# Retention and gated MLP on one core: mask and query scale built on the chip, two groups' totals interleaved with the next scores, one written order for all engines

## The chip, the cores and the metric

One core of one Trainium2 chip. The metric is the device time of one execution in microseconds (us); lower is better. TensorE (PE in the rows, its weight loads PEld) multiplies matrices, VectorE (DVE), ScalarE (ACT) and GpSimd (POOL) work on elements, SyncE (SP) issues the loads.

## The reference

For 4 batches, 8 heads, 768 positions and head size 64, a retention layer, then a gated MLP:

```python
for t in range(S):
    state = gamma * state + k[t] (outer) v[t]
    y[t] = (1 / sqrt(D)) * q[t] @ state
x = heads of y side by side                      # [4, 768, 512]
h = relu(x @ w_in); u, v = h[:512], h[512:]
v_n = (v - mean(v)) / sqrt(var(v) + 1e-6)
v_s = w_spatial @ v_n + b_spatial                # over positions
out = (u * v_s) @ w_out
```

All of it is wanted in float32 precision; the kernel gets it from pairs of float32r numbers (a high part and a residue), three products for one.

## The kernel before, in words

**Retention.** The 768 positions of a batch are 6 groups of 128; 4 batches give groups 0 to 23. A group has two halves i of 64 positions, and its 8 heads lie as 4 pairs, the two heads of a pair on partitions 0 to 63 and 64 to 127. `load_group` (L261) loads keys and queries (tile `qk`, 3 buffers), `load_values` (L273) values and natural keys (`vk`, 2 buffers; for groups 2, 5 and 8 `third`). `scale_values` (L289) multiplies the values by a decay from `vd_t`, in one POOL instruction or in 8 of ACT. `ret_scores` (L330) makes scores s = k'q in 16 products of 64x64, each two matmul records; `ret_mask` (L337, DVE) applies the causal mask `mask_t`. `total_sum` (L303) adds k'v of a half to a running total in PSUM (tile `total`, 8 products, 16 records), and `total_copy` (L318, ACT) copies the total to `states`. `out_products` (L381) makes x from scores and state (64 records for a group), `out_evict` (L408, DVE) takes it from PSUM in 4 instructions with the query scale `qg_t`, `qd_t`; `out_half` makes the high part `xh` (ACT) and the residue `xl` (POOL or DVE). x of groups 0 to 5 is written to the pool `ps_o`, whose three banks also hold the total. After group 5, `ret_set` (L342) alternates the scores of the next group with the update of the state, without a running total.

**MLP.** `v_products` (L456) makes v for one group and one quarter of the weights (3 matmuls of 512 columns), then `v_relu`, `v_stats`, `v_power`, `v_bias`, `mlp_norm` give the normalised `vn` (ACT, DVE, POOL). `mlp_u` (L579) makes u (12 matmuls), `spatial_products` (L598) multiplies vn by w_spatial (tile `sp`), `mlp_out` (L641) makes the output. Batch 0 multiplies in plain or split form, batches 1 to 3 by seven products (`product`, L540).

**Weights.** Twelve blocks of float64 words (L0 to L3 for v, L4 to L7 for u, L8 to L11 for the output) are loaded by `load_double` (L146) and taken apart: `split_top` on ACT, five DVE instructions (L181 to L204), `split_high` on ACT, `split_residue` (two instructions, POOL or DVE). Blocks 3 to 11 are staged in rooms that they share: L9 takes the room of L4.

**Order.** `START` (L24) is a string of words; while it is emitted, every instruction of every engine keeps this order. A word is a step and a number: q scores, j mask, p scale, t total, k copy, y output products, E eviction, h and l the halves of x, V products for v, r s w n N the norm, u, P spatial, G, L, K loads, a c H R the taking apart of a weight block. p23 scales group 3 on ACT, p1 group 1 on POOL. `FIRST`, `REST` and `LAST` (L37 to L57) give the order of batches 0 to 3; there only PE, the loads and the weight splits keep it, and a planner orders the rest. Before `START` ten matmuls on zeros run (`WARM_UP`, L738).

Of the kernel before, what the change touches and what calls it, by code (L numbers as in the profile page):

```python
# [9 lines left out]
F32 = mybir.dt.float32  # L10
# [13 lines left out]
START = (  # L24
# [10 lines left out]
)  # L35
FIRST = (
    "S6 W0 I4 W1 D1 X6 J9 S7 G9 D2 I5 X7 J10 G10 D3 W2 S8 W3 I6 X8 S9 V0 G11 W4 I7 X9 J11 S10 "  # L37
    "G12 O7 N0 X10 W5 V1 V2 V3 N1 N2 J12 G13 S11 X11 J13 G14 V4 N3 S12 N4 V5 W6 N5"
)
REST = (  # L40
# [4 lines left out]
)  # L45
LAST = (
    "U0 U2 C01 U4 C05 U6 C06 U1 U3 C03 M01 C07 M05 C02 M06 C04 M03 M07 M02 C11 M04 C15 F0 F2 O0 "
    "C16 O2 U5 U7 C13 M11 C17 M15 C12 M16 C14 M13 M17 M12 M14 F1 F3 O1 F4 O3 F6 O4 F5 O6 F7 O5 "
    "O7"
)  # L50


STAGED = {3: 0, 4: 1, 5: 2, 6: 3, 7: 4, 8: 0, 9: 1, 10: 2, 11: 3}
ROOMS = (12, 13)
# [769 lines left out]
```

## Time and profile before

| | us |
|---|---|
| median of 3 runs (lowest, highest) | 375.12 (374.98, 376.07) |
| span of the profiled execution, first to last instruction | 372.8 |
| PE busy in the span | 362.0 |
| DVE / ACT / POOL busy | 236.4 / 154.5 / 134.4 |

The profile gives one execution by its span; what lies around the span is known only as the difference of 2.3 us to the median. PE is the busiest engine by far, so the time is PE's work plus the time in which PE waits or runs at a lower clock. The chain that ended last, the windows (busy time of each engine in a stretch, with the granted clock) and the waits show where those are.

### The profile page before, as it was taken

How to read it: one execution, taken by the hardware profiler on the slowest of the kernel's cores; microseconds unless marked ns; L12 is line 12 of the kernel's file. 1: busy time of each engine (PE TensorE's matmuls, PEld its weight loads, DVE VectorE, ACT ScalarE, POOL GpSimd, SP SyncE). 2: the span in 40 equal slices, each digit the busy share in tenths (PEclk: the TensorE clock that was granted, in tenths of full speed). 3: DMA queues.
4: the chain of work that ended last, by engine and by line, in shares of the span. 5: the costliest groups of instructions: out<-in, count | busy, mean ns of one | idle time of the engine just before them, and what ended most of it. 6: DMA issues, size and time to landing. Idle time of an engine off the chain costs nothing.

```text
span 372.8 us, 10291 instructions
## 1 busy us (share of the span) xinstructions
PE 362.0 (97%) x4418; PEld 317.3 (85%) x4418; DVE 236.4 (63%) x513; ACT 154.5 (41%) x308; POOL 134.4 (36%) x131
## 2 busy tenths in 40 slices
PE   6899999999999999999999999999999999999996
PEld 2778785787998878999998888999997888999985
DVE  3989989995887876677674543367674433165530
ACT  2486682264433535533124444432323445432232
POOL 1354650001343523526424451327424341325042
PEclk9899999999999999999999999999999999999999
DMA  7997783001431721113305332021504002000022
GB/s 265 411 371 278 243 310 156 0 2 54 147 114 58 273 89 69 54 61 109 122 2 199 114 114 86 8 106 47 185 0 143 2 2 86 0 0 2 0 86 85
DMA packets 13581, 41.49 MB, mean 111 GB/s; under 512 B 1888, under 2 KB 2144, under 8 KB 13536
## 3 DMA queue, kind: packets, MB, share of 16 engines
q1 hardware_dynamic: 13392, 40.71, 30.0%
q8 instruction: 35, 0.57, 0.6%
q10 hardware_dynamic: 144, 0.13, 0.1%
q14 instruction: 10, 0.08, 0.1%
HBM read 34.54 MB, written 6.29 MB: 110 GB/s over the span
## 4 chain that ended last, share of the span: by engine, by line
PE 94%; DMA 3%; issue 1%; DVE 1%; POOL 0%; SPq 0%; ACT 0%; POOLq 0%
PE u L126 18%; PE v L126 18%; PE o L126 18%; PE y L126 10%; PE sp L126 8%; PE x L126 7%; PE z L126 5%; PE s L126 3%; PE d L126 3%; PE w L126 3%; DMA qk<-in_groups_dram 2%; DMA vd_t<-in_vdecay_dram 2%; PE total L126 1%; PE o_last L126 0%; POOL vk L298 0%
## 5 line engine op out<-in xcount | busy, mean ns | idle before, releaser
L126 PE MATMUL u<-xh,winu_w 128*128 128x384 f32 x256 | 68.1, 338 | 0.0
L126 PE MATMUL v<-winv_w,xh 128*128 128x512 f32 x192 | 60.6, 397 | 0.2 <-issue 0.2
L126 PE MATMUL o<-wout_w,gh 128*128 128x512 f32 (+1 forms) x192 | 60.5, 396 | 0.0
L126 PEld LDWEIGHTS u<-xh,winu_w 128*128 128x128 f32 x256 | 46.5, 188 | 0.8
L126 PE MATMUL u<-xl,winu_w 128*128 128x384 f32 x128 | 42.9, 335 | 0.0
L134 POOL TENSOR_TENSOR xl<-xf,xh 128x512 fp32r<-128x512 f32 x21 | 29.0, 1380 | 37.6 <-ACT xh L436 37.6
L126 PEld LDWEIGHTS v<-winv_w,xh 128*128 128x128 f32 x192 | 35.2, 188 | 8.1 <-issue 0.4
L126 PE MATMUL y<-sp,a 128*128 128x384 f32 x216 | 41.6, 336 | 0.0
L126 PEld LDWEIGHTS o<-wout_w,gh 128*128 128x128 f32 x192 | 35.2, 188 | 7.3
L534 ACT CAST a<-vn 128x384 fp32r<-128x384 f32 x42 | 21.6, 513 | 46.0 <-PE y L126 16.9
L134 POOL TENSOR_TENSOR gl<-ur,gh 128x384 fp32r<-128x384 f32 x24 | 26.8, 1116 | 37.7 <-ACT gh L630 37.2
L134 DVE TENSOR_TENSOR a<-vn,a 128x384 fp32r<-128x384 f32 x42 | 24.4, 580 | 24.6 <-ACT a L534 24.2
L126 PEld LDWEIGHTS y<-sp,a 128*128 128x128 f32 x216 | 38.1, 188 | 0.2
L126 PE MATMUL v<-winv_w,xl 128*128 128x512 f32 x96 | 37.5, 390 | 0.0
L126 PE MATMUL o<-wout_w,gl 128*128 128x512 f32 (+1 forms) x96 | 37.3, 389 | 0.0
L477 DVE BATCH_NORM_STATS2 bst<-vr 128x6 f32<-128x512 f32 x24 | 16.6, 691 | 29.3 <-ACT vr L470 29.1
L419 DVE SCALAR_TENSOR_TENSOR xf<-x,qg_t,qd_t 128x128 f32<-128x128 f32 x96 | 27.1, 343 | 10.3 <-PE x L126 10.3
L484 POOL TENSOR_TENSOR rs<-rs,mhalf 128x1 f32<-128x1 f32 x24 | 13.7, 573 | 44.0 <-DVE rs L479 41.8
L126 PE MATMUL s<-qk 64*64 64x64 f32 x768 | 27.4, 221 | 0.7 <-DMA qk<-in_groups_dram 0.7
L126 PEld LDWEIGHTS s<-qk 64*64 64x64 f32 x768 | 25.1, 137 | 2.9 <-DMA qk<-in_groups_dram 1.4
L500 ACT ACTIVATE vn<-vr,nb,rs 128x512 f32<-128x512 f32 x24 | 19.4, 814 | 17.4 <-DVE nb L489 16.4
L595 ACT ACTIVATE ur<-u 128x384 f32<-128x384 f32 x32 | 15.7, 490 | 25.9 <-PE u L126 25.7
(103 smaller groups left out, 669.8 us busy)
## 6 DMA issues: line engine op xcount, KB each, us to landing
qk<-in_groups_dram SPq DMA_DIRECT2D x24, 512.0 KB, 5.3
vk<-in_groups_dram SPq DMA_DIRECT2D x21, 512.0 KB, 4.4
out_dram<-ot SPq DMA_DIRECT2D x23, 256.0 KB, 2.1
wst<-in_w_sp_dram SPq DMA_DIRECT2D x4, 576.0 KB, 8.1
raw<-in_w_inv_dram SPq DMA_DIRECT2D x4, 512.0 KB, 6.5
raw<-in_w_inu_dram SPq DMA_DIRECT2D x4, 512.0 KB, 7.5
raw<-in_w_out_dram SPq DMA_DIRECT2D x4, 512.0 KB, 5.1
third<-in_groups_dram SPq DMA_DIRECT2D x3, 512.0 KB, 6.0
```

The lines of the kernel that those rows point to most:

```text
L126: ins = nc.tensor.matmul(out, lhs, rhs, start=start, stop=stop, skip_group_check=shared)
L134: return eng.tensor_tensor(out, whole, high.bitcast(F32), ALU.subtract)
L419: nc.vector.scalar_tensor_tensor(xf[:, hp], t[hp % 2][:, hp // 2].rearrange("p i c -> p (i c)"), qg_t[:, c, hp : hp + 1], qd_t[:, hp], ALU ...
L477: keep(nc.vector.bn_stats(st, norm[b, c][0]))
L484: keep(nc.gpsimd.tensor_tensor(rs, rs, mhalf, ALU.pow))
L500: keep(nc.scalar.activation(vn[b][:, c], v, AF.Identity, bias=nb, scale=rs))
L534: nc.scalar.copy(t[:, 0], whole)
L595: keep(nc.scalar.activation(u, pu[:, :HALF], AF.Relu))
```

## The change

Mask: built by POOL (memset and two affine selects) instead of loaded. Query scale: two rows are loaded, spread over 128 partitions by one float32 matmul with a 0/1 matrix, and copied by ACT (m2, m0, m1) instead of loaded whole (256 KB). `vd_t` and `qg_t` come in one load. Totals of groups 3 and 4 alternate with the scores of groups 4 and 5 (t130, t131, t140, t141). The total is written on the other half of the partitions and copied by two instructions of 64 partitions (k000, k001, ...). Filler matmuls on zeros: 11 at the start and eight more between steps (words U). Functions of several instructions are cut into steps of one engine each, and one string, `STEPS`, orders every instruction of the whole kernel; no planner is left. Numbers of the words change (p202: group 2 on ACT; R100: first residue instruction of block 0 on DVE; Q0: its second on POOL; E00: first eviction of group 0; x600: one addition to the state). From the v products of group 12 on, PE's order is that of before; ahead of it, in batch 0, it is changed.

```diff
-    "L0 G0 a0 c00 c01 H0 v c02 m q0 L2 j0 p0 t00 k00 y00 y01 t01 R20 G1 L1 p1 a2 G2 c20 E0 q1 "
-    "h0 k01 c21 j1 t10 y10 a1 H2 k10 G3 c10 y11 p22 t11 c22 q2 c11 k11 c12 L3 l0 H1 q3 t20 k20 "
-    "E1 G4 R1 V00 j2 h1 t21 l11 p23 k21 y20 y21 L5 R2 j3 q4 t30 E2 a3 h2 j4 c30 V10 p24 V01 V11 "
-    "V02 L4 l12 c31 V20 a5 k30 y30 c32 t31 H3 k31 c50 G5 y31 q5 E3 t40 a4 j5 R3 V21 V12 k40 c40 "
...
+    "U10 U301 G0 v q0 U201 j0 m2 m0 L0 a0 c00 c01 c02 p0 t00 m1 k000 k001 y00 U101 G1 p1 q1 "
+    "j1 H0 c03 R100 t01 y01 U501 E00 E02 c04 E01 Q0 E03 k010 k011 t10 k100 k101 t11 U401 U701 "
+    "U601 L1 a1 c10 L2 y10 G2 k110 k111 a2 y11 c11 c20 c21 E10 c22 q2 j2 c12 E12 E11 E13 p202 "
+    "t20 U801 k201 k200 c13 c14 h0 l0 G3 t21 H2 k210 k211 G4 h1 l101 H1 R101 p203 y20 y21 E20 "
+    "E21 Q1 q3 j3 c23 t130 k301 V00 V10 V11 k300 t131 E23 E22 p204 k310 k311 j4 c24 R2 Q2 h2 "
+    "l102 y30 y31 E30 E32 L3 G5 L4 t140 k401 k400 a3 c30 E31 c31 p205 a4 c32 H3 E33 h3 c33 "
+    "c34 R103 V20 V21 V01 V02 V12 V22 l103 t141 k410 y40 y41 E40 E41 E42 j5 E43 L5 k411 a5 "
+    "c50 c51 c52 G6 q6 G7 t50 k501 k500 Q3 V03 r0 V23 r2 V13 V30 V31 V32 h4 l4 c40 c41 c42 H4 "
+    "j6 s0 c43 R4 y50 p206 y51 c53 S6 E50 E51 E53 E52 h5 c54 A0 e0 c44 Q4 x600 V40 V41 V42 "
+    "V43 V33 l105 r1 V50 V51 V52 s2 s1 A1 L6 x601 a6 c60 w0 n0 H5 R5 e1 w1 A2 e2 w2 N0 r3 V53 "
+    "u0 Q105 n2 n1 p7 s3 A3 K3 L9 a9 K0 L8 N2 r4 N1 r5 e3 c61 s4 A4 s5 w3 a8 c80 A5 e5 n3 e4 "
+    "w4 c90 c91 N3 n4 N4 w5 n5 N5 u1 z0 z1 L10 K1 P1 c62 c92 c81 c93 x610 c82 H6 c63 c94 R106 "
...
-    def total_sum(g, i):
+    def total_sum(g, i, with_scores=False):
         if not total:
             total[0] = ps_o.tile([P, NP, D], F32, tag="o", name="total")
+        if with_scores and i == 0:
+            marks[g + 1] = bank(f"s{g + 1}")
         for hp in range(NP):
             for r in range(2):
-                rows = place(hp, r)
+                if with_scores:
+                    score(g + 1, i, hp, r)
+                rows, other = place(hp, r), place(hp, 1 - r)
                 mm(
-                    total[0][rows, hp],
+                    total[0][other, hp],
...
-    def total_copy(g, i):
+    def total_copy(g, i, r):
         dst = states[g][:, 1] if i == 0 else states[g + 1][:, 0]
-        keep(nc.scalar.copy(dst, total[0]))
+        keep(nc.scalar.copy(dst[ROWS[r]], total[0][ROWS[1 - r]]))
...
-        "m": lambda b, g, n: load(mask_t, mask),
-        "v": lambda b, g, n: [load(vd_t, vdecay), load(qg_t, qgroup), load(qd_t, qdecay)],
+        "m": lambda n: (decay_spread, decay_copy, decay_rows)[n](),
+        "v": lambda n: load(decay_t, decay),
+        "U": lambda n: warm(n % 100),
...
-    for i in range(WARM_UP):
-        nc.tensor.matmul(wps, wz[:, :P], wz, start=True, stop=True)
+    def warm(n):
+        for _ in range(n):
+            keep(nc.tensor.matmul(wps, wz[:, :P], wz, start=True, stop=True))
...
+    pick_t = slot(ROOMS[0], F32, "pick").rearrange("p s c -> p (s c)")[:, :P]
+    rows_t = slot(ROOMS[1], F32, "rows").rearrange("p s c -> p (s c)")[:, : NP * P]
+    nc.vector.memset(rows_t, 0.0)
+    nc.gpsimd.memset(pick_t, 0.0)
+    for r in ROWS:
+        nc.gpsimd.memset(pick_t[r.start : r.start + 1, r], 1.0)
+    nc.gpsimd.memset(mask_t, 1.0)
+    for r in ROWS:
+        nc.gpsimd.affine_select(
+            mask_t[r], mask_t[r], [[1, C]], ALU.is_ge, 0.0, base=0, channel_multiplier=-1
+        )
+    def decay_rows():
+        load(rows_t[::D], qdecay)
+    def decay_spread():
+        spread[0] = ps_m.tile([P, NP * P], F32, tag="m", name="spread")
+        mm(spread[0], pick_t, rows_t, True, True)
+    def decay_copy():
+        keep(nc.scalar.copy(qd_t.rearrange("p h c -> p (h c)"), spread.pop(0)))
```

## Rows read from the trace of the kernel before

**Rows 1.** The page, part 4: the chain that ended last, by engine.
```profile
PE 94%; DMA 3%; issue 1%; DVE 1%; POOL 0%; SPq 0%; ACT 0%; POOLq 0%
```
**Rows 2.** Windows: stretch, length, busy us (x instructions) by engine, granted clock, DMA, GB/s.
```profile
8.00:10.00 2.00, 0.70 (x22) 0.70 (x26) 1.68 (x4) 0.00 (x0) 1.25 (x1) 0.91 0.95 343
10.00:12.00 2.00, 2.00 (x65) 1.97 (x60) 1.41 (x3) 0.95 (x2) 0.00 (x0) 0.50 1.03 420
12.00:14.00 2.00, 1.69 (x40) 1.55 (x38) 1.97 (x7) 0.83 (x2) 0.88 (x1) 0.74 1.03 420
...
40.00:60.00 20.00, 20.00 (x159) 16.07 (x152) 17.41 (x45) 13.73 (x29) 10.84 (x12) 1.00 0.88 319
60.00:80.00 20.00, 20.00 (x81) 14.58 (x80) 18.83 (x36) 6.94 (x13) 0.00 (x0) 1.00 0.01 2
```
**Rows 3.** Waits of PE over the span: us in total, times, longest.
```profile
PE total L126 <- POOL vk L298: 3.0, 2, 2.0
PE x L126 <- issue: 1.4, 3, 0.6
```
**Rows 4.** The chain that ended last: start, us, what.
```profile
2.11 5.63 DMA vd_t<-in_vdecay_dram
...
22.57 1.16 PE x L126 x61
...
24.81 0.47 PE total L126 x16
...
33.77 1.09 PE x L126 x64
...
41.56 8.43 PE v L126 x36
49.99 4.18 PE u L126 x24
54.18 15.48 PE sp L126 x48
```
**Rows 5.** Timeline of the first 18 us: start, us, engine; in brackets the idle time before.
```profile
1.19 4.45 PE L738 MATMUL wps<-wz 128*128 128x512 bf16 x10 [1.19 <-DVE wz L735]
...
4.86 0.66 ACT L178 ACTIVATE room<-raw 128x512 f32<-128x512 f32 x1 [2.84 <-DMA raw<-in_w_inv_dram]
...
6.17 1.15 PE L126 MATMUL s<-qk 64*64 64x64 f32 x32 [0.53 <-DMA qk<-in_groups_dram]
...
7.88 1.37 POOL L298 TENSOR_TENSOR vk<-vk,vd_t 128x512 f32<-128x512 f32 x1 [7.05 <-DMA vd_t<-in_vdecay_dram]
...
12.21 1.48 PE L126 MATMUL s<-qk 64*64 64x64 f32 x32
...
17.54 2.02 ACT L295 ACTIVATE third<-third,vd_t 128x64 f32<-128x64 f32 x8 [1.73 <-DMA third<-in_groups_dram]
```
**Rows 6.** Groups by line and shape: count, busy us, mean ns, idle before.
```profile
L320 ACT COPY ws<-total 128x256 f32<-128x256 f32 x7 | 2.6, 366 | 4.5 <-PE total L126 4.5
L371 ACT COPY ws<-d 64x256 f32<-64x256 f32 x6 | 2.2, 368 | 0.6 <-PE d L126 0.6
...
L668 ACT COPY ot<-o 128x512 f32<-128x512 f32 x23 | 13.3, 584 | 8.1 <-PE o L126 7.1
...
L340 DVE TENSOR_TENSOR ws<-s,mask_t 128x512 f32<-128x512 f32 x21 | 14.3, 681 | 0.3 <-DMA mask_t<-in_mask_dram 0.3
...
L108 POOL MEMSET mhalf<- 128x1 f32 x1 | 0.1, 98 | 0.3 <-POOLq L809 0.3
```
**Rows 7.** Timeline: two DVE instructions beside POOL's, and ACT's last normalisation of batch 0.
```profile
28.95 1.30 POOL L134 TENSOR_TENSOR df<-df,winv_w 128x512 f32<-128x512 f32 x1 [2.96 <-ACT winv_w L207]
29.04 1.50 DVE L184 TENSOR_SCALAR room<-room 128x512 f32<-128x512 f32 x1
...
33.50 0.41 DVE L184 TENSOR_SCALAR room<-room 128x512 f32<-128x512 f32 x1
...
52.68 1.64 ACT L500 ACTIVATE vn<-vr,nb,rs 128x512 f32<-128x512 f32 x2 [1.17 <-DVE nb L489]
```

More of the change, by code (lines that the diff above doesn't have):

```diff
@@ L340, in ret_mask, with updated, set_products @@
         keep(nc.vector.tensor_tensor(d, s, mk, ALU.mult))
-    def ret_set(g, update=True):
-        nxt = g + 1 < NG
-        upd = [update and 0 <= g < NG, update and 0 <= g < NG and g % NC < NC - 1]
-        if not nxt and not any(upd):
-            return
-        first = True
+    changes = {}
+    def updated(g):
+        return 0 <= g < NG, 0 <= g < NG and g % NC < NC - 1
+    def set_products(g):
+        nxt, upd = g + 1 < NG, updated(g)
         if nxt:
@@ L351, in ret_set @@
         if any(upd):
-            change = bank(f"d{g}")
+            change = changes[g] = bank(f"d{g}")
         for i in range(2):
@@ L356, in ret_set @@
                     for r in range(2):
-                        score(g + 1, i, hp, r, pin=not first)
-                        first = False
+                        score(g + 1, i, hp, r)
                 if upd[i]:
@@ L362, in ret_set, with set_add @@
                         ops = naturals[g][rows, i, hp], values[g][rows, i, hp]
[L363 to L377 removed]
+                        mm(change[other, i, hp], *ops, start=True, stop=True)
+    def set_add(g, i, r):
+        dst = states[g][:, 1] if i == 0 else states[g + 1][:, 0]
+        u = changes[g][ROWS[1 - r], i]
+        if g % NC == 0 and i == 0:
+            keep(nc.scalar.copy(dst[ROWS[r]], u))
+        else:
+            keep(nc.vector.tensor_tensor(dst[ROWS[r]], u, states[g][ROWS[r], i], ALU.add))
     outs = {}
     def out_products(g, i):
[L382 removed]
+        b, c = divmod(g, NC)
         if i == 0:
[L384 removed]
+            pool, tag = (ps_o, "o") if b == 0 else (ps_m, "m")
             outs[g] = [
@@ new lines, in part_sum, with part_whole @@
+    def part_sum(b, p, m):
+        a11, a12, a21, a22 = corners(b, p)
+        keep(
+            nc.gpsimd.tensor_tensor(
+                *{
+                    7: (a11, a11, a21, ALU.subtract),
+                    5: (a21, a21, a22, ALU.add),
+                    6: (a21, a22, a11, ALU.subtract),
+                    3: (a21, a12, a21, ALU.subtract),
+                }[m]
+            )
+        )
+    def part_whole(b, p, m):
+        a11, a12, a21, a22 = corners(b, p)
+        return {1: a11, 2: a12, 4: a22, 7: a11}.get(m, a21)
@@ L538, in tile_retention_gmlp, with part_high, part_low @@
+    def part_high(b, p, m):
+        t = pieces[p, m] = pair_room(F32R, f"a{b}_{p}_{m}")
+        keep(nc.scalar.copy(t[:, 0], part_whole(b, p, m)))
+    def part_low(b, p, m):
+        t = pieces[p, m]
+        keep(residue(nc.vector, t[:, 1], part_whole(b, p, m), t[:, 0]))
     held = {}
+    bank_of = {1: "y", 6: "y", 7: "y", 4: "y", 5: "z", 3: "z", 2: "w"}
     def product(b, p, m):
-        bank_of = {1: "y", 6: "y", 7: "y", 4: "y", 5: "z", 3: "z", 2: "w"}[m]
         if m in (1, 5, 2):
-            held[bank_of] = ps_m.tile([P, DM], F32, tag="m", name=f"{bank_of}{b}_{p}")
@@ new lines, in mlp_out, with pieces_of, store @@
+            for k, (l, r) in enumerate(((gh, wout_h), (gh, wout_l), (gl, wout_h))):
+                at = dict(start=(first and k == 0), stop=(last and k == 2))
+                mm(o, l[:, col], r[:, j, c], **at)
+    def pieces_of(b, half):
+        whole = [(i, 0, slice(0, DM)) for i in range(TT)]
+        if (b, half) == (B - 1, 1):
+            i = whole.pop()[0]
+            whole += [(i, 0, slice(0, DM // 2)), (i, 1, slice(DM // 2, DM))]
+        return whole
+    def store(b, half, n):
+        i, n, c = pieces_of(b, half)[n]
+        o = acc[b, half][i + n][:, c]
+        rows = slice(half * HALF + i * P, half * HALF + i * P + P)
+        if n:
+            ot = rpool.tile([P, NP, P], F32, tag="xf", name="ot_last")
+            ot = ot.rearrange("p h c -> p (h c)")
+        else:
+            ot = mpool.tile([P, DM], F32, tag="v", bufs=3, name=f"ot{b}_{half}_{i}")
+        keep((nc.vector.tensor_copy if n else nc.scalar.copy)(ot[:, c], o))
+        keep((nc.scalar if n else nc.sync).dma_start(out[b, rows, c], ot[:, c]))
```

393 lines of the change are left out of this document (159 added, 234 removed), and 61 rows, old and new, of tables (REST, START, STEPS).

## The prediction

> **What bounds the kernel now.** I read the chain first: PE holds 94% of it [rows 1]. The windows then say where PE is not full. Between 40 and 80 us it is busy 20.00 of 20.00 twice [rows 2]: there an order can lose time but not win any, since the number of matmuls stays. What there is to win lies ahead of 40 us. The first real matmul starts at 6.17 [rows 5]; PE waits 3.0 us in two places for scaled values from POOL, and 1.4 us in three places that show no releaser ("issue") [rows 3]; and the granted clock falls to 0.50 in the window from 10 to 12 and averages 0.91 and 0.74 in its two neighbours [rows 2], after PE had done little from 7.3 to 9.3. At half of 2.4 GHz that lost 0.09x2 + 0.50x2 + 0.26x2 = 1.7 us. The last thing to see is how full DVE is: 17.41 of 20 and 18.83 of 20 us from 40 to 80 [rows 2]. If PE moves forward, DVE must follow.
>
> Only the span is known of the profiled execution; the median of the runs is 2.3 us above it. I work out a change of the span and take it off 375.1.
>
> **The loads at the start.** SP now issues keys and queries of group 0, its values, the decay, two short rows, and only then L0. The first load of before landed by 4.8 and the second by 6.1 (ACT and PE started on them at 4.86 and 6.17 [rows 5]); these places now belong to the keys and the values. The decay, which held POOL until 7.74 (2.11 + 5.63 [rows 4]), comes right behind, at about 6.3. Removed are 0.29 MB of query scale and mask, in small pieces. At the 420 GB/s of the following windows this is 0.7 us; the window from 8 to 10 moved only 343 GB/s [rows 2], and 2.0 us is the most I would give it. I take 1.7: the values of group 2 come at 15.8, where ACT had them at 17.5 [rows 5].
>
> **Mask and scale on the chip.** POOL gets three memsets of a tile or a row and two selects of 64 columns, a form that the trace lacks. Bounds: 0.10 us each (a memset [rows 6]) and 1.4 each (a 128x512 product [rows 5]), for all of it 0.6 to 8 us. POOL idles until 6.3, so even at 0.8 each nothing shows; the mask wait of 0.3 us on DVE [rows 6] goes. A gain is excluded, POOL was idle. I take nothing; the upper end would add 1.5. The spreading matmul is a plain float32 product like those of `sp`: 15.48 us for 24 products of 384 columns [rows 4] is 0.65 each, so 0.86 for 512. Its copy on ACT costs 0.58 [rows 6] ahead of the first total's copies and lies beside the scores of group 1.
>
> **PE to the end of x of group 0.** Fillers: ten took 4.45 us [rows 5], eleven take 4.7, from 1.19 to 5.9. Keys are there, so scores run 5.9 to 7.05, a filler to 7.25, the spread to 8.1. POOL scales the values from 6.4 to 7.8 (1.37 [rows 5]). Total, first half of x and a filler end at 9.1, scores of group 1 (loaded by then) at 10.2, second total and second half of x at 11.2. Before, these same steps end at 13.7, with the scores of group 1 (12.21 + 1.48 [rows 5]). The lead is 2.5 us, the larger part of it the half clock that the fillers and the spread keep away.
>
> **From there to 25 us the lead shrinks.** A total's copy becomes two instructions, and one of 64 partitions takes 368 ns as one of 128 takes 366 [rows 6]: eleven copies add 4.0 us to ACT. Total and copy take turns on one bank, so 0.3 of each pair lies on PE's path where nothing fills it. ACT scales group 2 from 15.8 for 2.02 us [rows 5], so its total starts at 17.9; x of group 2 also waits for DVE, which does nine instructions of L1 and L2 in between, and ends at 21.5. Before, it ended at 23.7 (22.57 + 1.16 [rows 4]), with the scores of group 3 (1.1) and one v step (0.7) done as well: the lead is 0.4. Then ACT has four copies, two h and two H before the scaling of group 3, which ends at 23.5. PE waits for it about one us, and total 3 starts where it did (24.81 [rows 4], less the scores around it).
>
> **Interleaving.** A total of a half alone takes 0.47 us for 16 records [rows 4], the scores of a group 1.15 for 32 [rows 5]. Where both use all four quarters of the array, as x does, 64 records take 1.09 [rows 4], 17 ns each instead of 29 to 36. So four totals cost 4x0.47 = 1.9 us before and nothing now. Those of group 3 fall partly into the wait just named; those of group 4 lie in full PE. With v steps (0.23 us a matmul by 8.43 us for 36 [rows 4]) filling PE from 24.8, x of group 4 ends at 34.7. The steps done then end at 34.9 + 0.70 + 0.47 = 36.0 before (one v step and one total more): a lead of 1.3. Up to x of group 5, at 41.6, PE is full in my count; before, the same steps end at 41.56 and 9 more v matmuls, 43.7. The lead is 2.1 us.
>
> Here a rule of the Trainium skill speaks against the change. "TensorE: Matmul & The Clock Gate", section "Part 3: Packing small matmuls", lets a weight load overlap a running matmul only if their row groups differ, and in t130 each total follows a score on the same rows. By it the 1.9 us would not be gained. The order of x has the same rows twice running in every second step and reaches 17 ns, so the trace speaks against the rule, and I count the gain.
>
> **What is late next.** The scores and update of group 6 move ahead of v (1.06 us, moved and not added); the update waits for ACT's scaling of group 6, which stands behind an H that waits for DVE: 0 to 0.8 us. The spatial products need all six normalised groups. Before, the last was ready at 54.3 (52.68 + 1.64 [rows 7]) and needed at 54.18 + 5x0.65 = 57.4, 3.1 us of room. DVE has more to do by then (one residue of x, one masking, three instructions of L8 and L9, about 4 us at 0.4 to 0.68 [rows 6, 7]) and starts later, since L0 does. My count puts the last normalisation at 56.9 to 58.1, the need, with the moved 1.06, at 57.4 + 1.06 - 2.1 = 56.4 to 58.5: 0 to 1.7 us are at risk. On SP, L9 now waits for the room of L4 with K0, L8, L10 and K1 queued behind it: DVE is through with L4 near 45, five loads of 2.7 MB at 400 GB/s end near 54, K1 is needed near 56. I take both waits as zero, because my steps are rounded up (28 us of DVE, some 5%).
>
> From group 12's v on, PE's order is that of before and its work the same; ACT, DVE and POOL get a fixed order. PE was full there between 40 and 80 us [rows 2], so a gain is excluded; a wait would cost in full, with a bound only as large as the second rival's. I take no change, as the steps stay those of before.
>
> Sum: 375.1 - 2.1 = 373.0. If the lead of 2.5 stayed and the interleaving came on top, 375.1 - 4.4 = 370.7.
>
> **Rivals.** First, the lead is eaten: the queues of ACT and DVE end the waits in place of the loads, PE idles for S6 (0.8) and the spatial products (0.9 or more), and 2.1 becomes about 0.3: 374.8. For it speaks that DVE was 94% busy there; against it, that nothing of DVE's stopped PE before. 0.25.
>
> Second, slower: DVE beside POOL. A `TENSOR_SCALAR` that took 0.41 us alone took 1.50 next to a POOL product [rows 7]. I counted two such meetings up to the last normalisation of batch 0; the order has some 25 of these instructions, and six more meetings add 6.5 us, of which 4 reach the last normalisation. It decides from 58.5 us on: there the old lead in work is gone, and each us later is one us lost. At 60.6 the time is 377.2. Against it: the long copies leave POOL idle between. 0.12.
>
> Third, the interleaving gives nothing. Then the two totals in full PE, 0.9, come back, and the two others as far as they were won: 375.1 - 2.1 + 1.3 = 374.3. It is the quoted rule as a mechanism of this kernel; the x rows leave it 0.03.
>
> **Chances and range.** My forecast, a gain of 1.2 to 4.4 us: 0.60. Within 0.3% (1.1 us, about what a measurement can tell from no change): the first and third rival, 0.28. Slower: 0.12. The range goes from 370.7, the undiminished sum, to 375.8, which takes in the first rival with both waits in full; it leaves out the slower rival and little else.
>
> **What would show it.** Right: no window at half clock; POOL's first product done by 8.0; x of group 0 ended by 11.5; t130 with its scores in 0.55 us; u of batch 0 starting at about 49 with group 6's update behind it; PE idle by under 8 us in all. Wrong: PE idle of over 1 us before the first `sp` released by ACT or DVE; a half-clock window in spite of the fillers, worth up to 1.7; POOL's selects ending after 6.4; a wait in batches 0 to 1 where PE was full.

## The result, and the profile after

The changed kernel takes 379.37 us (median of 4 runs, 377.88 to 380.51) against 375.48 for the kernel before on the same chip: the ratio is 1.0113 (95% interval 1.0078 to 1.0148), slower by 3.9 us. In a second set of runs it was 1.0084 (1.0058 to 1.0109). The forecast was 373.0, and its range ended at 375.8. The profiled execution after took 379.78 with a span of 377.9; before, the span was 372.8.

First the windows of after, with the columns of [rows 2] (for each engine busy us and instructions, then granted clock, DMA share, GB/s):

```profile
12.00:14.00 2.00, 0.92 (x48) 0.87 (x45) 1.90 (x4) 1.08 (x3) 0.30 (x1) 1.00 1.04 416
14.00:16.00 2.00, 0.77 (x18) 0.67 (x20) 2.00 (x6) 1.13 (x4) 0.22 (x1) 1.00 0.96 369
16.00:18.00 2.00, 2.00 (x19) 0.84 (x19) 1.39 (x3) 1.72 (x4) 1.05 (x1) 0.57 0.76 299
18.00:20.00 2.00, 2.00 (x73) 1.93 (x74) 0.86 (x3) 2.00 (x9) 0.00 (x0) 0.58 0.11 37
...
150.00:200.00 50.00, 49.52 (x640) 45.47 (x643) 38.26 (x77) 16.36 (x34) 17.09 (x18) 1.00 0.18 65
```

The half-clock stretch of before, at 8 to 14 us [rows 2], has not gone: it lies at 16 to 20, after two windows in which PE was busy 0.92 and 0.77 of 2 us, and takes (0.43 + 0.42) x 2 = 1.7 us of clock again. The last row looks harmless, 49.52 of 50 us (50.00 of 50 before), and yet 2 us are lost in that stretch, as the table below shows: the busy share alone does not tell.

The waits of PE, to be held against [rows 3]:

```profile
PE total L155 <- ACT ws L353: 1.7, 2, 0.9
PE total L155 <- issue: 1.5, 1, 1.5
PE wps L716 <- DVE wz L776: 1.2, 1, 1.2
PE d L155 <- POOL vk L327: 1.1, 1, 1.1
PE v L155 <- DVE xl L161: 1.0, 1, 1.0
PE total L155 <- ACT third L353: 0.9, 1, 0.9
PE s L155 <- DMA qk<-in_groups_dram: 0.5, 1, 0.5
PE z L155 <- DVE xf L450: 0.4, 1, 0.4
```

The 3.0 us for POOL's scaled values at the start are gone, as forecast (the 1.1 us for them lie at group 17), and ACT has taken their place. Why, the timeline of the start shows:

```profile
1.50 0.52 POOL L788 TENSOR_SCALAR_AFFINE_SELECT mask_t<-mask_t 64x64 f32<-64x64 f32 x2
6.05 1.15 PE L155 MATMUL s<-qk 64*64 64x64 f32 x32
6.14 1.04 POOL L327 TENSOR_TENSOR vk<-vk,decay_t 128x512 f32<-128x512 f32 x1 [4.12 <-DMA decay_t<-in_decay_dram]
7.36 1.02 PE L155 MATMUL spread<-rows,pick 128*128 128x512 f32 x2
8.52 1.28 ACT L201 ACT_TABLE_LOAD   x1 [8.52 <-DMA raw<-in_w_inv_dram]
9.82 0.67 ACT L201 ACTIVATE room<-raw 128x512 f32<-128x512 f32 x1
10.39 0.57 ACT L800 COPY qd_t<-spread 128x512 f32<-128x512 f32 x1
10.97 0.75 ACT L353 COPY ws<-total 64x256 f32<-64x256 f32 x2
11.77 0.51 PE L155 MATMUL total<-vk 64*64 64x64 f32 x10 [0.88 <-ACT ws L353]
```

The table load of 1.28 us, which before ran unseen at 0.73 us, now waits for the first weight block and stands in front of everything that ACT does. The scratch of the query scale (`pick_t` and `rows_t`) lies in the rooms into which the first splits write, so the first activation has two things to wait for, its load and the spreading matmul; one of the two waits was put on the table load ahead of it. In the run `mended` below, where that scratch lies elsewhere, the table load runs at 0.79.

Where the time went is read from TensorE's start at the same step in both traces (first weight load of the step; us later than in the profiled execution before; one profiled execution of each run). "u 1.2" is the u product with number 2 of batch 1, `u12` in the written order; group 12 is the first of batch 2. At the last three columns TensorE has done the same steps in both orders; at the first u product, the scores and update of group 6 (1.1 us) are done in addition in the new order.

| run | first u 0.0 | u 1.2 | v of group 12 | u 2.0 | ratio to before (95%) |
|---|---|---|---|---|---|
| changed | +3.28 | +1.01 | +3.23 | +4.54 | 1.0113 (1.0078-1.0148) |
| after_again | +2.81 | +0.53 | +2.83 | +3.21 | 1.0084 (1.0058-1.0109) |
| before_onchip | +0.66 | +0.69 | +0.62 | +0.64 | 1.0008 (0.9988-1.0027) |
| table_first | +1.28 | -0.11 | +2.09 | +2.74 | 1.0098 (1.0081-1.0114) |
| s6_pool | +0.99 | -1.05 | +1.22 | +2.05 | 1.0056 (1.0035-1.0077) |
| no_interleave | +6.42 | +4.29 | +6.53 | +6.89 | 1.0161 (1.0127-1.0196) |
| p17_early | +1.96 | +0.04 | +2.30 | +3.01 | 1.0096 (1.0080-1.0111) |
| by_hand | +1.54 | -0.70 | +1.52 | +2.10 | 1.0052 (1.0036-1.0068) |
| planner_b1 | +3.00 | +3.36 | +7.17 | +7.99 | 1.0217 (1.0204-1.0230) |
| mended | -0.04 | -1.85 | +0.67 | +0.87 | 1.0033 (1.0021-1.0046) |
| b1_before_only | +1.91 | -0.37 | +2.81 | +2.81 | 1.0036 (1.0022-1.0050) |
| b1_before | -0.05 | -2.07 | -0.23 | -0.22 | 0.9999 (0.9987-1.0010) |
| b1_before_c24 | +0.50 | -1.70 | +0.31 | +0.34 | 0.9994 (0.9975-1.0014) |
| products_before | +2.17 | +0.06 | +5.50 | +5.52 | 1.0114 (1.0086-1.0142) |
| m101_before | +0.43 | -1.40 | +5.49 | +5.54 | 1.0116 (1.0087-1.0146) |
| best | +0.14 | -1.84 | +5.13 | +5.12 | 1.0104 (1.0082-1.0126) |
| b1_all_only | +1.10 | +6.75 | +6.76 | +6.76 | 1.0178 (1.0139-1.0217) |
| b1_all_before | +0.15 | +5.42 | +6.94 | +6.97 | 1.0155 (1.0117-1.0193) |
| visits | +1.13 | -0.76 | +3.01 | +3.60 | 1.0071 (1.0056-1.0087) |

In the changed kernel the start costs 3.28 - 1.1 = 2.2 us, the rest of batch 0 wins 1.2, batch 1 loses 2.2 more up to the v products of group 12, and the products of group 17 lose 1.3. From there on TensorE loses nothing more (+4.56 at the v products of group 18); the last 0.5 of the 5.1 us by which the span is longer lie behind its last product.

Two things can be read down the columns. The start varies: in the eight runs that leave all up to the first u product as in the changed kernel (changed, after_again, p17_early, by_hand, planner_b1, b1_before_only, products_before, b1_all_only) it is late by 1.10 to 3.28 us there; in the five with its two mends and no other edit of the start (mended, b1_before, m101_before, b1_all_before, visits) by -0.05 to 1.13. The profiled execution of the changed kernel is the worst of the eight. The loss in batch 1 does not vary: from u 1.2 to the v products of group 12 it is 2.2 to 2.3 us in the six runs that keep the written order there (changed, after_again, table_first, s6_pool, no_interleave, p17_early) and 2.2 and 2.5 in the two that move single steps of the other engines (by_hand, mended), with u 1.2 anywhere from -1.85 to +4.29. So it does not follow from the start.

### The profile page after: what moved, and what is told of

Its sections match the earlier page's. It is cut to its first block, busy times and chain, and to the rows that moved or that the text cites. A ratio compares the mean times of both kernels' runs of the same rounds, so it can differ in the third digit from the quotient of the medians.

```text
span 377.9 us, 10336 instructions
## 1 busy us (share of the span) xinstructions
PE 364.9 (97%) x4425; PEld 316.9 (84%) x4428; DVE 238.7 (63%) x521; ACT 157.4 (42%) x320; POOL 124.3 (33%) x130
## 4 chain that ended last, share of the span: by engine, by line
PE 88%; DVE 4%; ACT 3%; DMA 1%; issue 1%; SPq 0%; POOL 0%; DVEq 0%; POOLq 0%; ACTq 0%
PE o L155 18%; PE u L155 17%; PE v L155 16%; PE y L155 10%; PE sp L155 8%; PE x L155 6%; PE z L155 5%; PE d L155 3%; PE w L155 2%; PE s L155 2%; DMA raw<-in_w_inv_dram 1%; ACT vk L324 1%; ACT ws L353 1%; DVE xf L450 1%; PE total L155 1%
## 5 line engine op out<-in xcount | busy, mean ns | idle before, releaser
L548 POOL TENSOR_TENSOR vn<-vn 128x384 f32<-128x384 f32 x24 | 26.2, 1092 | 60.1 <-DVE a L161 57.3
L161 POOL TENSOR_TENSOR gl<-ur,gh 128x384 fp32r<-128x384 f32 x22 | 23.8, 1081 | 39.9 <-ACT gh L664 39.4
L450 DVE SCALAR_TENSOR_TENSOR xf<-x,decay_t,qd_t 128x128 f32<-128x128 f32 x96 | 28.7, 344 | 10.4 <-PE x L155 7.1
L327 POOL TENSOR_TENSOR vk<-vk,decay_t 128x512 f32<-128x512 f32 x18 | 20.5, 1138 | 30.0 <-DVE sp L161 14.7
L155 PE MATMUL s<-qk 64*64 64x64 f32 x768 | 29.6, 221 | 0.5 <-DMA qk<-in_groups_dram 0.5
L664 ACT CAST gh<-ur 128x384 fp32r<-128x384 f32 x24 | 12.3, 513 | 40.4 <-DVE ur L599 20.8
L155 PEld LDWEIGHTS s<-qk 64*64 64x64 f32 x768 | 26.2, 134 | 3.4 <-issue 2.9
```

What stands on the lines that cost most here:

```text
L155: keep(nc.tensor.matmul(out, lhs, rhs, start=start, stop=stop, skip_group_check=shared))
L161: return eng.tensor_tensor(out, whole, high.bitcast(F32), ALU.subtract)
L327: keep(engine.tensor_tensor(values[g], values[g], vd, ALU.mult))
L450: nc.vector.scalar_tensor_tensor(xf[:, hp], t[hp % 2][:, hp // 2].rearrange("p i c -> p (i c)"), qg_t[:, c, hp : hp + 1], qd_t[:, hp], ALU ...
L548: nc.gpsimd.tensor_tensor(*{7: (a11, a11, a21, ALU.subtract), 5: (a21, a21, a22, ALU.add), 6: (a21, a22, a11, ALU.subtract), 3: (a21, a12, ...
L664: keep(nc.scalar.copy(gh, t))
```

## The experiments

Three theories went in: the loss has three separate places (start, batch 1, group 17); the start alone is the cause; TensorE's own new order in batch 1 is the cause. The last column above is each run against the kernel before on the same chip.

**Start: the table load.** The first edit gives ACT a tiny activation of its own.

```diff
+    ready = wpool.tile([P, 1], F32, name="ready")
+    keep(nc.scalar.activation(ready, mhalf, AF.Abs))
```

> The changed kernel with one activation of 128x1 on a constant as ScalarE's first work, so that the table load has no wait of its own. Theory (the loss has three places, and one is the start: the table load stands behind the landing of the first weight block, 1.28 us on ScalarE's queue ahead of the decay copy and the copies of the running total): the first split activation begins near 8.5 instead of 9.82 us, everything behind it on ScalarE 1.3 us earlier, and the time falls by 0.9 to 1.4 us against the changed kernel, to about 378.2; if the half-clock stretch of 16 to 20 us goes with it, by up to 2.8. Rival 1 (the start alone is the cause, and the waits of batch 1 follow from it): the time falls by 3 us or more, to 376.5 or less. Rival 2 (VectorE's late chain of the weight split sets the start, not ScalarE): less than 0.3 us.

ACT's timeline of this run:

```profile
0.79 1.28 ACT L156 ACT_TABLE_LOAD   x1 [0.79 <-PEq L872]
2.08 0.20 ACT L156 ACTIVATE ready<-mhalf 128x1 f32<-128x1 f32 x1
8.62 0.68 ACT L205 ACTIVATE room<-raw 128x512 f32<-128x512 f32 x1 [6.33 <-PE spread L159]
9.20 0.58 ACT L804 COPY qd_t<-spread 128x512 f32<-128x512 f32 x1
```

The first split starts at 8.62 for 9.82, 1.2 us earlier, and now shows its true releaser, the spreading matmul. The half-clock stretch is gone. By the first u product 2.0 us are won (1.28 for 3.28), but 1.28 lies among the eight unedited starts above, and the time, 1.0098, lies between the two sets of the changed kernel. The theory holds in its mechanism; that this edit alone gains time is not shown, and the start is not the whole cause.

**Start: group 6's values.**

```diff
-h4 l4 c40 c41 c42 H4 j6 s0 c43 R4 y50 p206 y51
+h4 l4 p6 c40 c41 c42 H4 j6 s0 c43 R4 y50 y51
```

> The changed kernel with the value scaling of group 6 made on GpSimd in one instruction of about 1.04 us, straight after the low part of group 4's output, in place of eight on ScalarE (2.02 us) that stand behind the high half of a weight block. Theory (TensorE waits about 1.2 us for these values at the products of group 6): the update products there run without the wait, and the time falls by 0.9 to 1.2 us against the changed kernel. Rival 3 (the wait moves, because the evictions and statistics that follow on VectorE and ScalarE are late too): less than 0.4 us.

What it removes is seen in these rows of the changed kernel's timeline:

```profile
42.12 1.29 POOL L161 TENSOR_TENSOR xl<-xf,xh 128x512 fp32r<-128x512 f32 x1 [3.85 <-ACT xh L467]
...
43.99 0.62 ACT L235 CAST winu_w<-df 128x512 fp32r<-128x512 f32 x1 [1.95 <-DVE df L219]
44.52 2.02 ACT L324 ACTIVATE vk<-vk,decay_t 128x64 f32<-128x64 f32 x8
...
42.19 1.77 DVE L219 SCALAR_TENSOR_TENSOR df<-raw,room 128x512 int32<-128x512 int32 x1
```

A DVE step that takes 0.68 us alone (at 20.26 us) took 1.77 beside POOL's product; ACT's high half waited for it, the scaling stood behind that half, and the set of group 6 took 2.35 us from start to start where the set of group 14 takes 1.09. In this run the set takes 1.50 us, 0.85 less, and TensorE is 0.99 late at the first u product: the theory holds, in size too, as far as the varying start lets one say.

**Interleaving undone.**

```diff
-t130 ... t131 ... t140 ... t141
+q4 t30 ... t31 ... q5 t40 ... t41
```

> The changed kernel with the running total of groups 3 and 4 again separate from the next groups' scores: the scores first, then the total, in the same places. Theory (interleaving is not where the time went: 32 records of a pair take 0.46 to 0.55 us without waits where 16 of the scores alone take 0.92): 0.5 to 1.5 us slower than the changed kernel. Rival 4 (interleaving ties the scores to the total's waits on ScalarE and costs what it saves): within 0.3 us of it, or faster.

1.0161 against 1.0084 to 1.0113: 1.8 to 2.9 us slower. PE ran into half clock at 34 to 38 us here, and not at 16 to 20. The theory holds; the price is above its range.

**Before, with the new loads alone.** The order of before is kept; the mask is made by GpSimd, the two decays come in one load, and the query scale is spread by a matmul.

```diff
-        "m": lambda b, g, n: load(mask_t, mask),
-        "v": lambda b, g, n: [load(vd_t, vdecay), load(qg_t, qgroup), load(qd_t, qdecay)],
+        "e": lambda b, g, n: decay_spread(),
+        "v": lambda b, g, n: [load(decay_t, decay), load(rows_t[::D], qdecay)],
```

> The kernel before with only the loads changed: mask made on GpSimd, one load for the two decays, the query scale spread by a matmul with its copy, the scratch of it in buffers of its own; its order of steps stays. Theory (making them on the chip is no loss, and the three loads that go were ahead of the first values): faster than the kernel before by 0.3 to 1.5 us, 374.0 to 375.2. Rival (the spread matmul and its copy, or GpSimd's memsets and selects, delay the start by themselves): slower than the kernel before by 0.5 to 1.5 us.

```profile
8.19 1.09 POOL L296 TENSOR_TENSOR vk<-vk,decay_t 128x512 f32<-128x512 f32 x1 [6.20 <-DMA decay_t<-in_decay_dram]
...
9.34 0.68 PE L124 MATMUL total<-vk 64*64 64x64 f32 x16 [1.74 <-POOL vk L296]
9.95 1.12 PE L124 MATMUL spread<-rows,pick 128*128 128x512 f32 x2
```

No change: 1.0008 (0.9988 to 1.0027). POOL's first product, at 7.88 before [rows 5], starts at 8.19: 0.29 MB less to load bring nothing as long as the decay stands behind the same loads. That it starts at 6.14 in the changed kernel is due to the order of the loads alone. Both sides missed.

**Group 17, and batch 1 with single steps moved.**

```diff
-J17 j17 h15 x1600 l15 Z100 x1601 x1610 Z101 x1611 f16 V120 p17
+J17 p17 j17 h15 x1600 l15 Z100 x1601 x1610 Z101 x1611 f16 V120
```

> The changed kernel with the value scaling of group 17 put ahead of the low part of group 15's output on GpSimd's list, straight after its load; nothing else is moved. Theory: the wait of TensorE for the scaled values (1.1 us at the products of group 17) goes and nothing stands behind it, so the time falls by 0.9 to 1.3 us against the changed kernel. Rival (the wait only moves: the low part of group 15 comes 1.04 us later and holds the output buffers of group 17, or the output matmuls wait instead): within 0.3 us.

From the v products of group 12 to u 2.0, 0.71 us are lost for 1.31, but the second profile of the changed kernel lost 0.38, and the time, 1.0096, lies between its two sets: no gain is shown. The scaling cannot start much earlier, since its load lands late (in the run with ten moved steps POOL waits 6.22 us for it, to 205.32).

> The changed kernel with TensorE's order, the loads and the spatial weight splits as written throughout, but from group 12 on the order of all other steps of ScalarE, VectorE and GpSimd left to the planner, as in the kernel before. Theory (the written order of the three engines in batch 1 costs 1.9 us between groups 12 and 15 and 1.3 us at group 17): the time falls by 2 to 3.3 us against the changed kernel, to 376.1 to 377.4. Rival (TensorE's own new order in batch 1, with group 13's output matmuls ahead of the product of the second corner, is the cause): within 0.5 us of the changed kernel.

```diff
-    keep = tc.keep_in_program_order
+    def keep(ins):
+        if not free:
+            tc.keep_in_program_order(ins)
...
+        if word == "S12":
+            free.append(True)
```

Slower, 1.0217: the planner, fed with the new order of steps, does worse than the written one (PE waits 1.6 us at one place for ACT's casts). It is not the plan of before; both forecasts missed, and the run decides nothing.

> The changed kernel with TensorE's order untouched and only ten steps of batch 1 moved on ScalarE's, VectorE's and GpSimd's lists: the residue of the first half's last corner ahead of two additions on VectorE; the low parts of the first two gates from VectorE to GpSimd; the high and low parts of the outputs of groups 12, 13 and 14 straight after the outputs are evicted; the last two evictions of group 14 ahead of the next half's additions; the value scaling of group 17 after its load. Theory (the written order of these three engines in batch 1 is the loss there): the 2.1 us between the u product 1.2 and the output product 1.3, and the 0.6 to 1.3 us at group 17, come back: 2.2 to 3.3 us less than the changed kernel, 376.1 to 377.2 us. Rival 2 (TensorE's own new order in batch 1 is the cause): within 0.8 us, of which 0.6 is group 17's.

The moves: `b104` behind `b107`; `d110 d112` made `d10 d12`; `h12` behind `C104`, `l12` behind `T115`; `h13` behind `z15`, `l13` behind `p15`; `E143 E142` behind `E141`, `h14 l14` behind `C113`; `p17` behind `J17`. They answer to these rows of the changed kernel (timeline of DVE and POOL), which I took for the cause:

```profile
175.36 2.64 DVE L161 TENSOR_TENSOR gl<-ur,gh 128x384 fp32r<-128x384 f32 x2
...
202.07 1.13 DVE L450 SCALAR_TENSOR_TENSOR xf<-x,decay_t,qd_t 128x128 f32<-128x128 f32 x4 [3.13 <-POOL xl L161]
```

The time, 376.86, lies in the theory's range, and yet the theory falls. Both jams are gone, and between u 1.2 and the v products of group 12 TensorE still loses 1.52 + 0.70 = 2.2 us, as much as unedited (3.23 - 1.01 = 2.2). What the run won (1.0052) lies ahead of u 1.2, in a start that it did not edit, and at group 17 (0.58). A wait that is seen and can be removed need not be one that costs.

**Three edits at once**: scratch in other buffers, which also leaves the table load without a wait, group 6's values on GpSimd, and the moved steps.

```diff
-    pick_t = slot(ROOMS[0], ...
-    rows_t = slot(ROOMS[1], ...
+    pick_t = slot(10, ...
+    rows_t = slot(11, ...
```

> The changed kernel with three edits at once: the scratch of mask and query scale in buffers that no weight block waits for (so that the table load has no wait), group 6's values scaled on GpSimd, and the ten moved steps of batch 1. Theory (three separate places, whose costs add): 2.0 + 1.0 + 2.7 us less than the changed kernel, 373.0 to 374.5, which is faster than the kernel before by 1 to 2 us. Rival 1 (the start alone is the cause): what the other edits bring overlaps with the start, and the sum is not over 3 us, 376 us or more.

The ratio is 1.0033; the time, 376.31, is the rival's. But the rival's reason is not: the start now has what was expected (-0.04 at the first u product, in spite of the 1.1 us of group 6 done ahead); batch 1 again loses 0.67 + 1.85 = 2.5 us, and PE shows no wait of over 0.2 us in it. At the start TensorE still waits 2.6 us for ACT's copies of the total and its scaling (1.1, 0.9 and 0.6); the waits of before have no such row. What the copy in two instructions costs was not run by itself.

**Batch 1 in the old order.** All steps of all engines between u 1.2 and the first v product of group 12 in the sequence of the trace before; for the second run with the mended start.

> The changed kernel with all steps between the u product 1.2 and the first product of group 12's v, on every engine and TensorE among them, in the order in which the kernel before ran them; ahead of it and behind it the changed order. It differs from the run with ten moved steps in TensorE's order above all, which has two fewer changes between wide fp32r products and the 64x64 products there. Theory as the ten moved steps left it (1.0 us of the loss in batch 1 was the three engines' lists, and the 2.5 us that stay without a wait of over 0.2 us come from TensorE's own order): 1.5 to 2.5 us less than with the ten moved steps, 374.4 to 375.4 us. Rival 5 (those 2.5 us come from what batch 0 left behind on the engines, and follow any order): within 0.7 us of the ten moved steps, 376.2 to 377.5.

> The run with three edits at once, with the order of the kernel before in batch 1 (as in the run beside it) in place of the ten moved steps: scratch of mask and scale in buffers of its own, group 6's values scaled on GpSimd, batch 1 in the old order on all engines. Theory (the places are separate and TensorE's order in batch 1 costs about 2.2 us): 373.5 to 374.5 us, faster than the kernel before by 0.5 to 1.5 us. Rival 5 (batch 1's stalls follow from batch 0): 375.5 to 376.5.

The second reaches the kernel before, 0.9999. In it TensorE loses 1.6 us between u 1.2 and the first product of batch 1 (-2.07 to -0.43) and nothing from there on (-0.23 at the v products of group 12). The first gives 1.0036; there the loss moved ahead too (-0.37 to +0.99), and 1.2 us more went on a late load of keys. By its time the first is the rival's, the second stands between theory and rival. The old order saves the products, and something already late when it begins takes time ahead of them (in the second run PE waits 1.1 us there for ACT's `ur`).

> The run beside it (buffers of its own, group 6 on GpSimd, batch 1 in the old order) with one more edit: the last step of weight block 2's split on VectorE and its sum on GpSimd stand behind the low part of group 2's output on VectorE, so that this VectorE product no longer runs beside a GpSimd product. Theory (a VectorE product of 128x512 takes 0.68 us alone and 1.75 beside GpSimd, and TensorE waits 1.0 us for it): the product takes 0.7 us, the wait of the v product is gone or under 0.3, and the time falls by 0.5 to 1.0 us. Rival (the length is that of the product, not of the neighbour): it still takes over 1.5 us and the time stays.

```diff
-c24 R2 Q2 h2 l102
+R2 h2 l102 c24 Q2
```

The rows of DVE and POOL without this edit, and then with it:

```profile
27.84 1.66 DVE L162 TENSOR_TENSOR xl<-xf,xh 128x512 fp32r<-128x512 f32 x1 [0.32 <-ACT xh L468]
...
27.66 1.28 POOL L244 TENSOR_TENSOR winv_w<-df,room 128x512 fp32r<-128x512 f32 x1 [1.85 <-DVE room L233]
```

```profile
27.94 0.69 DVE L162 TENSOR_TENSOR xl<-xf,xh 128x512 fp32r<-128x512 f32 x1 [0.92 <-ACT xh L468]
...
29.67 1.28 DVE L207 TENSOR_SCALAR room<-room 128x512 f32<-128x512 f32 x1
...
29.38 1.29 POOL L244 TENSOR_TENSOR winv_w<-df,room 128x512 fp32r<-128x512 f32 x1 [3.47 <-DVE room L233]
```

The product alone takes 0.69 us, and PE's wait for it is gone: that half of the theory is shown. The time stays (0.9994, 0.9975 to 1.0014): POOL's product now stretches another DVE step (0.41 to 1.28), and the products of group 6 wait 1.1 us in its place.

**Where in batch 1?** The changed kernel again, and three with the old order only from the first spatial product (M101) on.

> The changed kernel itself, unedited, beside the runs it is compared with. Every theory: 1.007 to 1.015 of the kernel before, as the first time.

> The changed kernel with one edit: the steps of all engines from the first spatial product of batch 1 (1.0.1) to the first v product of group 12 in the order of the kernel before; everything ahead of it, the u products included, and everything behind it stays. Theory (the order of the products costs 1.9 us up to the output product 1.3, of which TensorE's part is 1.8 once the other engines are mended, and the place of group 17's scaling 1.3 more): 2.5 to 3.3 us less than the changed kernel, 376.1 to 376.9 us, and 0.3 to 0.7 us less than with the ten moved steps. Rival 5 (the stalls there are a consequence of batch 0 and follow any order): within 1.5 us of the changed kernel.

> The same edit together with the two mends of the start (scratch of mask and scale in buffers of its own; group 6's values on GpSimd). The run with three edits lost 1.8 us between the product 1.0.1 and the output product 1.3 without a wait of over 0.2 us; with the whole batch in the old order nothing was lost there, but 1.6 us ahead of it, where the u products' evictions came late. Theory (TensorE's own order of the products is the cause of the 1.8): both are avoided, 374.0 to 374.8 us, 0.997 to 0.9995 of the kernel before. Rival 5: 375.5 us or more.

> The run beside it with two more edits in the start: the last step of weight block 2's split and its sum behind group 2's low part (VectorE's product then runs alone and took 0.69 us in place of 1.66), and the masking of group 6's scores ahead of three steps of weight block 4 on VectorE's list. Theory (with the first edit alone the 1.0 us won at the v product came back as a wait of the products of group 6 for a bank of scores that VectorE had not yet masked): that wait is gone too, 0.5 to 1.2 us less than the run beside it, 373.0 to 374.0 us. Rival (VectorE is the bound from 28 to 42 us, and whatever is put first delays another step that TensorE needs): within 0.3 us of the run beside it.

The unedited kernel came out at 1.0084, in its range. The other three, forecast at 373.0 to 376.9 us, took 378.7 to 379.6. All three stall 3.3 us at one product (the waits of PE from 18 to 205 us, second run, `m101_before`):

```profile
PE y L156 <- DVE t L594: 3.3, 1, 3.3
```

The old order wants the parts of batch 1 (GpSimd's sums of quarters of vn, each cast by ACT and its residue taken by DVE before the next sum) earlier than the new order makes them. GpSimd's first four sums, before and in the changed kernel:

```profile
149.22 1.03 POOL L529 TENSOR_TENSOR vn<-vn 128x384 f32<-128x384 f32 x1 [2.20 <-DVE a L134]
150.32 1.21 POOL L532 TENSOR_TENSOR vn<-vn 128x384 f32<-128x384 f32 x1
152.97 1.01 POOL L532 TENSOR_TENSOR vn<-vn 128x384 f32<-128x384 f32 x1 [1.43 <-DVE a L134]
155.19 1.00 POOL L532 TENSOR_TENSOR vn<-vn 128x384 f32<-128x384 f32 x1 [1.22 <-DVE a L134]
```

```profile
149.58 1.27 POOL L548 TENSOR_TENSOR vn<-vn 128x384 f32<-128x384 f32 x1 [11.40 <-DVE a L161]
155.92 1.06 POOL L548 TENSOR_TENSOR vn<-vn 128x384 f32<-128x384 f32 x1 [0.23 <-ACT vn L526]
160.56 1.01 POOL L548 TENSOR_TENSOR vn<-vn 128x384 f32<-128x384 f32 x1 [3.59 <-DVE a L161]
162.79 1.02 POOL L548 TENSOR_TENSOR vn<-vn 128x384 f32<-128x384 f32 x1 [1.22 <-DVE a L161]
```

The last sum is 7.6 us later, where TensorE is 1 us late. The second waits for ACT's normalisation. Around that stall TensorE also falls to half clock in all three (windows of the second run, columns as above):

```profile
162.00:164.00 2.00, 0.00 (x0) 0.00 (x0) 1.97 (x4) 1.44 (x4) 0.17 (x1) 1.00 0.00 0
164.00:166.00 2.00, 1.21 (x4) 1.24 (x5) 1.97 (x5) 0.00 (x0) 0.00 (x0) 0.53 0.00 0
166.00:168.00 2.00, 2.00 (x8) 2.00 (x7) 0.04 (x1) 0.00 (x0) 0.00 (x0) 0.50 0.00 0
168.00:170.00 2.00, 2.00 (x8) 2.00 (x7) 1.10 (x2) 0.51 (x1) 0.00 (x0) 0.50 0.01 4
```

By my estimate from the length of these stretches while TensorE worked, that is 1.7, 3.1 and 2.9 us. Of the 5.4, 6.9 and 7.0 us lost from u 1.2 to the v products of group 12, stall and half clock are then all but 0.4 to 0.7, where the new order loses 2.2 and more.

In the run `best`, the win at x of group 4 (0.7 us against `mended`) was gone at the first u product, where PE waited 1.0 us for ACT's `vr`: the stall moved a second time. Theory and rival of that run are not told apart by its time (1.0104 for 1.0116, each to about 0.0025).

> The changed kernel with one edit: all steps of all engines from the last v products of batch 1's group 8 to the first v product of group 12 in the order of the kernel before; the start and batches 2 and 3 as changed. Here the parts of batch 1 are prepared in the old order too, which the run from the first product on did not have (there TensorE stood 3.3 us at one product for parts that came late). Theory (what batch 1 costs is the order of all engines within it, from the last normalisations on, and has nothing to do with the start): TensorE's lag against the kernel before stays what it is at group 8's v products (about +1.5 to +2 us on the un-mended start) up to the end, and the time is 2.4 to 3.2 us less than the changed kernel in the same call before, 1.001 to 1.003 of the kernel before. Rival 5 (batch 1 in the old order still loses 2 us or more, because it begins late on ScalarE, VectorE and GpSimd): 1.006 or more.

> The same edit with the two mends of the start (scratch in buffers of its own, group 6's values on GpSimd). Theory: the lead of 1.2 us that the mended start still has at group 8's v products stays to the end: 0.9965 to 0.9985 of the kernel before, 373.6 to 374.4 us. Rival 5: 1.001 or more.

Here the old order begins at the v products of group 8. By their times, 1.0178 and 1.0155, both runs missed the theory by far, as at the seam PE waits 4.7 us for DVE and then runs at half clock for 6.8 us. From u 1.2 on the first run stays at +6.75 to +6.76 over 54 us of batch 1: no loss at all. The second stays at +5.4 up to the products, and has one wait of 1.2 us for a load of keys after. That agrees with the theory, with one reservation: the stall and the slow stretch gave the other engines time to get ahead.

> The run with three edits, with two of TensorE's steps moved in batch 1 and nothing else but what hangs on them: the output products of group 13 stand behind the last product of the first half of the columns instead of ahead of it, and the score and update set of group 15 right behind the output products of group 14 instead of between the second and third product of the second half, so that wide fp32r products are interrupted by 64x64 products four times instead of six between the first product and group 14's update (the value scaling of group 15 goes ahead of two gate parts on GpSimd for it). Theory (each interruption costs TensorE time by itself, without a recorded wait: a wide step of 2.02 us takes 2.34 where a 64x64 step follows, and a product of 1.56 takes 1.70 where one stands before): 2 x 0.45 us less than the run with three edits, 0.6 to 1.1 us, 1.0005 to 1.002 of the kernel before. Rival (the time lies in late parts from the other engines, which a product meets wherever it stands): within 0.3 us of the run with three edits, 1.003 or more.

```diff
-M107 F102 F107 x1311 y130 y131 J15 G16 O107 M104 S14
+M107 F102 F107 x1311 O107 M104 y130 y131 J15 G16 S14
-j15 E140 O102 x1410 E141 E143 E142 z17 M111 F111 M115 x1411 S15
+j15 x1410 x1411 S15 E140 O102 E141 E143 E142 z17 M111 F111 M115
```

Slower than `mended`, 1.0071. With fewer changes of shape (from wide products to 64x64 steps and back) PE met the late parts openly:

```profile
PE y L156 <- DVE t L594: 0.8, 1, 0.8
PE z L156 <- DVE t L594: 0.8, 1, 0.8
PE x L156 <- ACT ur L626: 0.6, 2, 0.4
```

So the 64x64 steps between the products of the new order seem to cover waits for evictions and parts, and TensorE's order alone is not the cause. Nor is the start alone: the 2.2 us stay whatever it does. At group 17 five runs with the order unedited there (changed, after_again, table_first, s6_pool, no_interleave) lost 0.4 to 1.3 us. What share of the 2.2 us is the late chain and what share the two added changes of shape stays open; that chain alone, put earlier in an otherwise unchanged order, was not tried.

## Why the prediction was wrong

**Two steps failed.** One is the lead out of batch 0, "The lead is 2.1 us", from which the sum is made: at u 1.2 TensorE was 1.0 us behind the kernel before (0.5 in the second profile), where 2.1 ahead was forecast. These 3.1 us alone would have carried the time to 376.1, out of the range.

The other is "From group 12's v on, PE's order is that of before and its work the same ... I take no change, as the steps stay those of before". TensorE's order is indeed that of before from there on, but ahead of it more is changed than batch 0, which alone the description of the change names: in batch 1 neither PE's order was that of before nor the lists of ACT, DVE and POOL, and the prediction has no term for that stretch. Its ground, "PE was full there between 40 and 80 us", is a row of another stretch: group 12's v starts at 200.2 us before. A step that is the same is not the same wait. The text bounded it ("a wait would cost in full"), and then gave it no price and no chance of its own. What it left out cost 2.2 us in batch 1, and 1.3 (0.4 in the second profile) at group 17. None of the predicted rivals is this one.

**The start** was forecast at 49.61 - 2.1 + 1.1 = 48.6 for the first u product; it was at 52.89, 4.3 later. Three parts can be set against it: the table load together with the half clock, 2.0 (`table_first`); the set of group 6, 2.35 - 1.1 = 1.25, where I said 0 to 0.8 and took 0; and the wait for `xl` of group 2, 1.0, which stays in `mended`, whose first u product at 49.57 is 1.0 behind the forecast. Each size is that of single profiled executions, and this start varies by 2 us; the two groups of runs above show that the two mends together bring the start forward; the share of each they do not show. The step that missed the table load is "Mask and scale on the chip ... I take nothing": the engine times were right, and the buffers in which the scratch lies were not looked at.

**The half clock** was priced by its length, 1.7 us, as "the larger part" of the first lead. But before, TensorE still waited 1.0 us for POOL behind that stretch, and POOL for a load, issued at 6.14:

```profile
13.12 1.51 POOL L298 TENSOR_TENSOR vk<-vk,vd_t 128x512 f32<-128x512 f32 x1 [3.87 <-DMA vk<-in_groups_dram]
14.69 0.68 PE L126 MATMUL total<-vk 64*64 64x64 f32 x16 [1.00 <-POOL vk L298]
```

At full clock TensorE would have come to this total sooner and waited longer: what the stretch cost is less than the 1.7 us.

**The loads.** Scores at 5.9 were at 6.05, POOL's first product done by 7.8 was at 7.2: right (though eleven fillers at 4.45 us for ten are 4.9 and not 4.7; they took 4.87). But the gain is the order's; the 0.7 to 2.0 us for bytes removed are worth nothing in `before_onchip`.

**Right in size:** the selects (0.52 us for two, done at 2.0), the spreading matmul (1.02 for 0.86), and the interleaving: the second half of group 4's total with group 5's scores, 32 records, takes 0.46 us, 14 ns each (window of after, columns as above):

```profile
36.39:36.85 0.46, 0.46 (x30) 0.46 (x32) 0.46 (x2) 0.00 (x0) 0.24 (x1) 1.00 0.00 0
```

The rule of the Trainium skill ("TensorE: Matmul & The Clock Gate", "Part 3: Packing small matmuls") that was weighed there lets a weight load overlap a running matmul only if the row groups differ. The row speaks against it for this order, in which a total alone takes 0.47 [rows 4]. The waits for the last normalisation of batch 0 and for K1, taken as zero, did not appear.

**The slower rival** (DVE beside POOL, 377.2, a chance of 0.12) had the right mechanism at the wrong place: it met the low part of group 2 and the weight split ahead of group 6, not the last normalisation, with TensorE waiting 1.0 and about 1.2 us.

Batch 0 won 1.2 us behind the first u product that I had not counted (0.3 in `table_first`).

## What to carry to other kernels

When a change rewrites the order of all engines, each stage needs its own term, also the stages whose steps stay: compare the start of the same step in both traces, stage by stage, and ask which chain (here sums, casts and residues of the parts) has moved against TensorE. Before a scratch tile is put into a buffer that something else uses, ask who writes that buffer first. And a wait that the profile names is worth removing only if the work behind it can then run: in several runs here it moved on to the next engine.

## What the runs showed of the hardware

The table load ran where the first activation's wait was put: at 0.79 us with nothing to wait for, at 8.52 behind a load, each 1.28 us. "ScalarE activation tables: per-element evaluation and per-set limits" of the Trainium skill, section "What a function is on this engine", gives 1283 ns for one. The rows agree.

These DVE steps, which started while POOL worked on 128x512, were stretched by about as much as POOL still ran: 0.69 to 1.66, 0.68 to 1.77, 0.41 to 1.28. Not every step was: an eviction, which reads PSUM, took its 0.30 us beside POOL's product at 29.38. The Trainium skill, "GPSIMD Engine Reference", "8. Key points", says that GpSimd shares its SBUF interfaces with VectorE, in contention with VectorE's instructions of two SBUF inputs or in a 2-port mode. The two longest of these rows have two such inputs; for the third the trace does not tell the mode.

TensorE's clock was granted at half (1.2 GHz of 2.4) from 16.3 to 19.7 us in both profiles of the changed kernel, though single filler matmuls stood between its steps; in the two 2 us windows ahead it had been busy 0.92 and 0.77 us, and 0.87 and 1.13. In `no_interleave` the same came at 34.2, after 0.69 and 0.42. Yet `before_onchip` kept the full clock after a window from 14 to 16 us in which TensorE did nothing, so these rows give no rule.
